# Rows by parity in a two-headed state-space kernel: 64x64 pieces for kv's first stage, half-width matmuls for A's last, loads in halves and a new order

## The chip, the core and the metric

The kernel runs on one core of a Trainium2 chip. The core has five engines with a queue each: TensorE (PE, with its weight loads shown apart as PEld), VectorE (DVE), ScalarE (ACT), GpSimd (POOL) and SyncE (SP). SP and POOL issue nearly all transfers here. The metric is the device time of one execution in microseconds.

## The reference

Two independent heads share the output's columns, the first 1024 from A and the last 1024 from B; each works on 2048 rows of 1024 columns in bf16.

```
k_shift = sum over t of k_pad[:, t:t+S, :] * shift_k[:, 3 - t]      # 4 taps along the rows
kv  = k_shift * v
y   = irfft(rfft(kv padded to 4096) * rfft(ssm_k padded to 4096))[:S]
A   = q * (y + kv * ssm_D)

Bu  = x @ B_bar^T                                                   # complex, 1024 states
h_t = Lam_bar * h_(t-1) + Bu_t                                      # 2048 steps
B   = 2 * Re(h @ C^T) + x * Dskip
```

## The kernel before

**Head B** goes through 16 chunks i of 128 rows. `x.i` loads a chunk transposed; `U.i.jp.jl` are PE's 16 matmuls of a quarter-pair of Bu into a PSUM bank, and `ue.i.jp` (L466, ACT) casts a bank to SBUF. VectorE then multiplies by a rotation table (`r1`, L479), adds (`r2`, L486), runs the recurrence as two scans (`sc`, L492), rotates back with `r3` (L479) and `r4` (L498). Between chunks `cy.i` (L488, ACT) copies the last column of chunk i-1, as r4 left it, into chunk i; the scans of chunk i wait for it. `y.i.dh.part` are PE's output matmuls, four of 512 columns (L508) and one of 128 with the diagonal Dd (L511) in each part, eight parts a chunk; `ye` (L517) casts them and `yst` or `ysp` stores them from POOL or SP. Before the first chunk, `bl`, `bT`, `bc` (L437) bring B transposed into BT, `cl`, `cT`, `cc` (L445) or `cx` bring C into CT, and `z1` (L362) and `z2` (L365 to L367) write the rotation tables Z1 and Z2 on ACT; only r3 reads Z2.

**Head A** is a convolution by a transform of 4096 points in three stages of small matmuls. For each of 16 row phases n2, `kvm`, `kva`, `kvb`, `kvc` (VectorE) make kv from k, the taps and v. k sits in a ring of eight row slots that `kp.r` fills, two rows a time; `vp.r` and `qp.r` load v and q likewise. `am.n2.dh` (L563) is kv's first stage, `ae` (L569) its cast, `ast.n2` (L572) its store to the scratch Ys_kv from POOL. The filter goes the same way through `hl`, `hT`, `hc`, `hm` (L609), `he`, `hst` into Ys_h. Stage two works on 32 frequency groups g in pairs i: `lh.i`, `lk.i` (L629) and `lw.i` load, `sh.g` and `sk.g` (L640) transform, `she` (L649) and `ske` (L656) cast, `sw` and `swp` (L660) swap partitions by DMA from POOL or SP, `pr.i` (L666, VectorE) multiplies, `sa.g` (L678) transforms back, `sae` casts, `vst` stores to Vs. A load lk or lh needs all first-stage stores of its scratch, since each reads rows of all of them. The last stage reads Vs with `vl.n2`, transforms with `a3.n2.dh` (L706), casts with `a3e` (ACT) or `a3ev` (VectorE, both L713), multiplies by q with `qm.r` (L715, VectorE) and stores with `ost` or `osp` (POOL or SP).

Row 16m + s of k, v, q and A's output lies on partition m in slot s. The first stage wants even and odd m apart (p = 0, 1); before the change this is done by constants whose other rows, or columns, are zero:

```
F1 = np.stack([tr * (m % 2 == p)[:, None] for p in range(2)], axis=1)
G = np.stack([tr.T * (m % 2 == p)[None, :] * 2 / NFFT for p in range(2)], axis=1)
```

`am` is then two full 128x128 matmuls of 512 columns, one for each p, and `a3` two of them that accumulate in one bank. The filter's `hm` runs already as four 64x64 matmuls (constant FQ), two row halves by two column halves.

All of this is issued in one order, written out as a string of words, each a step of the above with the arena slots (a), PSUM banks (p), scan slots (h) and weight slots (w) that it takes. Every engine and every DMA queue runs its own steps in the order of the words; semaphores do the rest. SBUF is one arena of 53 units, handed out by hand, and so are the eight banks.

```
cur.setdefault(code, []).append(int(n))
...
E[f](*map(int, args))
```

Of the kernel before, what the change touches and what calls it, by code (L numbers as in the profile page):

```python
# [32 lines left out]
def a_constants():  # L33
# [5 lines left out]
    F1 = np.stack([tr * (m % 2 == p)[:, None] for p in range(2)], axis=1)  # L39
    FQ = np.concatenate([tr[::2], tr[::2]], axis=0)  # L40
    G = np.stack([tr.T * (m % 2 == p)[None, :] * 2 / NFFT for p in range(2)], axis=1)
# [23 lines left out]
    return f(F1), f(FQ), f(G), f(W)  # L65

ORDER = """
bl.0.1:a46 ld_par ld_w:a0 wb.3:p0 wbe.3:a20 bl.6.0:a32 par_T:p2 p32 exp1 dd wb.6:p4 wbe.6 wb.2:p2 ld_F wbe.2 kp.0:a12
bl.7.1:a42 bl.6.1:a43 wb.1:p1 bl.0.0:a35 wb.7:p3 wbe.7 wbe.1 wb.0:p7 bT.6.0:p4 gz x.1:a48 kring bc.6.0 wbe.0
bl.7.0:a25 kp.1 wb.5:p1 wbe.5 wb.4:p5 bl.1.0:a9 bT.0.1:p4 dve2 dve3 tabA1:a4a40a6a10 wbe.4 exp2 kp.-1 bT.6.1:p1  # L70
bT.0.0:p2 x.0:a49 bc.0.1 bT.7.1:p3 bl.2.1:a42 sm_pre sin0 bT.7.0:p5 rt bc.6.1 bc.0.0 bl.3.1:a24 tabA2 bl.1.1:a33
kvm.3:a26 U.1.3.0:a34p6 bT.1.0:p4 par_rest kva.3 U.1.0.0:p2 bc.7.1 bc.7.0 U.1.3.1 U.0.3.0:a8p0 U.0.3.1 kvm.1:a44
bT.2.1:p5 sin2 bl.2.0:a43 bl.3.0:a50 sin1 bT.3.1:p7 eo bc.1.0 kvb.3:a39 bT.1.1:p3 U.0.0.0:p1 bc.2.1 bl.5.0:a30 kva.1
kvm.2:a0 stt bl.5.1:a31 kva.2 bT.2.0:p4 bl.4.1:a38 bc.1.1 bT.3.0:p5 bl.4.0:a52 ue.0.3 U.1.0.1 U.0.0.1 bc.2.0 bc.3.0
bT.4.1:p3 bT.5.0:p0 ue.1.0 bT.4.0:p5 kp.-2 U.1.1.0:p2 bc.3.1 kvm.0:a26 bT.5.1:p4 bc.5.0 bc.4.1 kvb.1:a38 kva.0 bc.4.0
cl.2.0:a32 bc.5.1 ue.0.0 U.1.1.1 U.0.1.0:p0 x.2:a51 cT.2.0:p7 kvb.2:a36 ue.1.3 U.0.1.1 U.0.2.0:p4 vp.0:a42 U.0.2.1
# [19 lines left out]
ye.2.0:a48 hst.0.6.0 he.0.7.0.0 vp.4:a10 sc.3.0 y.2.1.0:p6 y.2.1.1 am.3.1:p5p0 hst.0.4.1 ae.3.0.1 y.2.1.2 y.2.1.3
sc.3.1 hst.0.5.0 am.4.1:p2p4 x.5:a34 ae.4.1.1:a6 hst.0.7.0 ye.2.1 ae.3.1.1 U.4.0.0:a32p7 U.4.3.0:p5 am.5.1:p1p0
kvm.6:a0 U.4.3.1 ae.5.0.1:a28 vp.3:a40 U.4.0.1 kvc.8 ast.3 ue.4.3 am.4.0:p1p3 ue.4.0 ae.4.1.0 ae.5.1.1 r3.3:a44
U.4.2.0:p4 kva.6 am.5.0:p3p5 U.4.2.1 ae.5.0.0 ae.4.0.0 am.8.1:p7p6 ae.4.0.1 am.8.0:p0p3 ae.8.1.0:a4 U.4.1.0:p1 r4.3
kvb.6:a35 yst.2 hst.0.5.1 ue.4.2 kvc.6 U.4.1.1 ae.8.1.1 ae.8.0.1 U.5.1.0:a30p3 kvm.9:a46 U.5.1.1 ae.5.1.0 y.3.1.0:p2  # L100
y.3.0.0:p6 am.6.1:p4p5 ast.4 y.3.0.1 kvm.7:a24 ue.5.1 am.6.0:p7p3 ae.6.1.0:a6 ue.4.1 ae.8.0.0 ae.6.1.1 ae.6.0.1
y.3.0.2 kva.9 y.3.0.3 kva.7 y.3.1.1 hm.0.1.1:p3p1 he.0.1.1.1:a38 hm.0.1.0:p4p5 he.0.1.0.1 ye.3.0:a35 he.0.1.1.0
he.0.1.0.0 ae.6.0.0 y.3.1.2 kvb.9:a36 kvb.7:a51 kvc.9 hl.3.1:a42 y.3.1.3 hl.3.0 ye.3.1 hl.2.1:a0 hl.2.0 U.5.2.0:p1
am.9.1:p6p3 ae.9.0.1:a8 ae.9.1.1 U.5.2.1 ue.5.2 hT.1.3:p2 kvc.7 ast.5 hc.1.3:a50 kp.5 r1.4:a46 am.7.0:p6p5 hT.1.0:p7
hst.0.1.0 ae.7.0.0:a32 ae.7.1.0 ast.6 kvm.11:a24 ast.8 am.9.0:p0p4 ae.9.1.0 r2.4:h0 kva.11 hc.1.0:a28 hT.1.1:p1
hT.1.5:p6 am.7.1:p5p2 hc.1.1:a29 ae.7.1.1 cy.4 sc.4.0 kvb.11:a40 U.5.3.0:p3 ysp.3 hd.1 ae.7.0.1 U.5.0.0:p4 ae.9.0.0
ast.7 kvm.10:a24 hst.0.1.1 sc.4.1 U.5.0.1 U.5.3.1 hc.1.5:a41 hm.1.1.0:p5p2 kva.10 hm.1.1.1:p0p7 x.8:a11 ue.5.0 kp.6
x.9:a36 U.8.0.0:a6p1 he.1.1.1.0:a46 hT.1.4:p0 hT.1.7:p6 he.1.1.0.1 U.8.3.0:p4 ue.5.3 hc.1.4:a51 he.1.1.1.1 vp.5:a48
x.6:a10 he.1.1.0.0 U.8.3.1 kvc.11 hT.1.2:p0 hc.1.7:a29 hT.1.6:p3 hm.1.7.0:p7p5 kvb.10:a37 he.1.7.0.1:a32 he.1.7.0.0
hc.1.2:a3 U.8.1.0:p2 U.8.1.1 ue.8.3 r3.4:a42 U.8.0.1 am.11.0:p6p5 U.6.1.0:a38p7 ae.11.1.0:a4 U.6.1.1 hc.1.6:a35 ue.8.0  # L110
ae.11.0.0 am.11.1:p3p4 U.6.3.0:p0 ue.6.1 ast.9 hst.1.1.0 vp.6:a0 hst.1.1.1 ue.8.1 ae.11.1.1 U.6.3.1 ae.11.0.1 ast.11
kvm.12:a24 hm.1.0.0:p1p5 hm.1.2.0:p6p7 hm.1.7.1:p2p4 he.1.7.1.0 r4.4 U.6.0.0:p3 he.1.7.1.1 he.1.0.0.0:a46 kva.12
# [78 lines left out]
def full_kernel(ctx, tc, A_q, A_k, A_v, A_shift_k, A_ssm_k, A_ssm_D, B_x, B_Lre, B_Lim, B_Bre, B_Bim,  # L191
# [590 lines left out]
```

## Time and profile before

| | |
|---|---|
| three runs | 357.69, 358.66, 360.29 us (median 358.66) |
| profiled execution | 358.65 us, of which the span is 356.8 us |
| mean granted TensorE clock | 0.990 |
| PE / DVE / ACT / POOL busy | 333.2 / 330.3 / 271.5 / 68.9 us |
| moved by DMA | 100.91 MB, 283 GB/s over the span |

The span runs from the first to the last instruction; busy time is the union of an engine's instructions. In a row of the timeline the columns are start, length, engine, line, operation, output and inputs, count, and in brackets the idle time just before it with what ended it. Successive instructions of an engine overlap a little in the records, so a difference of starts tells better than a length what one more instruction costs. A row of the waits gives the waiting engine and line, what it waited for, and total, times and longest in us.

### The profile page before, as it was taken

How to read it: one execution, taken by the hardware profiler on the slowest of the kernel's cores; microseconds unless marked ns; L12 is line 12 of the kernel's file. 1: busy time of each engine (PE TensorE's matmuls, PEld its weight loads, DVE VectorE, ACT ScalarE, POOL GpSimd, SP SyncE). 2: the span in 40 equal slices, each digit the busy share in tenths (PEclk: the TensorE clock that was granted, in tenths of full speed). 3: DMA queues.
4: the chain of work that ended last, by engine and by line, in shares of the span. 5: the costliest groups of instructions: out<-in, count | busy, mean ns of one | idle time of the engine just before them, and what ended most of it. 6: DMA issues, size and time to landing. Idle time of an engine off the chain costs nothing.

```text
span 356.8 us, 9113 instructions
## 1 busy us (share of the span) xinstructions
PE 333.2 (93%) x3745; PEld 223.9 (63%) x3785; DVE 330.3 (93%) x277; ACT 271.5 (76%) x512; POOL 68.9 (19%) x108
## 2 busy tenths in 40 slices
PE   5869989899999979999999999999999999999993
PEld 1769989444775868658574574655474777844441
DVE  4999899799999999999969999999999999999980
ACT  5999799897558984889667688898898997226540
POOL 5000020231612210561200020022130412000021
PEclk9998999999999998999999999999999999999999
DMA  7999899671988994787979889999999899899694
GB/s 224 326 279 310 248 242 281 194 253 44 298 294 317 282 260 177 193 312 222 348 246 311 305 303 275 317 366 320 359 303 344 319 314 327 296 355 386 204 401 154
DMA packets 62565, 100.91 MB, mean 283 GB/s; under 512 B 29438, under 2 KB 31502, under 8 KB 62524
## 3 DMA queue, kind: packets, MB, share of 16 engines
q1 hardware_dynamic: 52684, 66.60, 62.0%
q0 software_dynamic: 9840, 33.74, 26.0%
q8 instruction: 29, 0.48, 0.6%
q14 instruction: 12, 0.10, 0.1%
HBM read 52.08 MB, written 33.55 MB: 240 GB/s over the span
## 4 chain that ended last, share of the span: by engine, by line
PE 70%; DMA 12%; ACT 7%; issue 5%; SPq 3%; POOL 1%; DVE 1%; POOLq 0%; DVEq 0%
PE bank L508 25%; PE bank L461 24%; PE bank L640 4%; PE bank L678 4%; DMA arena<-in_B_x_dram 3%; DMA wslot<-a_c_W 3%; PE bank L706 3%; PE bank L563 3%; SPq L443 3%; ACT BT L437 2%; PE bank L609 2%; PE bank L511 2%; DMA arena<-Vs 2%; DMA CT<-in_B_C_im_dram 2%; PE bank L421 1%
## 5 line engine op out<-in xcount | busy, mean ns | idle before, releaser
L461 PE MATMUL bank<-arena,BT 128*128 128x128 bf16 x2048 | 129.2, 222 | 5.1 <-DMA arena<-in_B_x_dram 3.5
L461 PEld LDWEIGHTS <-BT 128*128 128x128 bf16 x2048 | 120.1, 99 | 19.5 <-issue 7.7
L508 PE MATMUL bank<-CT,gslot 128*128 128x512 bf16 x483 | 120.5, 379 | 3.0 <-issue 1.0
L492 DVE TENSOR_TENSOR_SCAN gslot<-rtab,gslot 128x1040 bf16<-128x1040 f32 x32 | 73.0, 2312 | 6.3 <-ACT gslot L488 6.2
L508 PEld LDWEIGHTS <-gslot 128*128 128x128 bf16 x512 | 44.5, 98 | 53.0 <-issue 8.7
L466 ACT CAST arena<-bank 128x512 bf16<-128x512 f32 x64 | 38.7, 623 | 19.5 <-PE bank L461 17.5
L569 ACT CAST arena<-bank 128x512 bf16<-128x512 f32 x64 | 35.9, 620 | 8.9 <-PE bank L563 8.7
L617 ACT CAST arena<-bank 128x512 bf16<-128x512 f32 x64 | 34.3, 616 | 6.9 <-PE bank L609 5.9
L666 DVE TENSOR_TENSOR arena<-arena 128x4096 bf16<-128x4096 bf16 x16 | 36.6, 2287 | 2.1 <-DMA arena<-arena 1.0
L479 DVE TENSOR_TENSOR arena<-arena,Z 128x4096 bf16<-128x4096 bf16 x16 | 36.5, 2284 | 1.1 <-ACT arena L466 1.1
L479 DVE TENSOR_TENSOR arena<-gslot,Z 128x4096 bf16<-128x4096 bf16 x16 | 36.6, 2286 | 0.4
L686 ACT CAST arena<-bank 128x512 bf16<-128x512 f32 x60 | 33.4, 610 | 4.4 <-PE bank L678 4.3
L656 ACT CAST arena<-bank 128x512 bf16<-128x512 f32 x58 | 33.0, 614 | 2.6 <-PE bank L640 2.4
L649 ACT CAST arena<-bank 128x512 bf16<-128x512 f32 x57 | 31.5, 615 | 4.4 <-PE bank L640 4.4
L620 POOL DMA_DIRECT2D Ys_h<-arena x32 | 23.3, 730 | 45.8 <-ACT arena L617 45.8
L517 ACT CAST arena<-bank 128x512 bf16<-128x512 f32 x31 | 18.8, 606 | 15.6 <-PE bank L511 15.6
L543 DVE TENSOR_TENSOR arena<-arena 128x4096 bf16<-128x4096 bf16 (+3 forms) x16 | 30.1, 1884 | 0.4 <-ACT arena L466 0.3
L511 PE MATMUL bank<-Dd,arena 128*128 128x128 bf16 x128 | 28.0, 219 | 0.2
L572 POOL DMA_DIRECT2D Ys_kv<-arena x16 | 11.2, 719 | 84.2 <-ACT arena L569 82.2
L660 POOL DMA_DIRECT2D arena<-arena x16 | 8.8, 553 | 82.9 <-ACT arena L649 44.9
L713 ACT CAST arena<-bank 128x512 bf16<-128x512 f32 x24 | 12.8, 597 | 12.1 <-PE bank L706 10.9
L511 PEld LDWEIGHTS <-arena 128*128 128x128 bf16 x128 | 12.5, 98 | 15.1
(102 smaller groups left out, 383.3 us busy)
## 6 DMA issues: line engine op xcount, KB each, us to landing
Ys_kv<-arena POOLq DMA_DIRECT2D x16, 512.0 KB, 5.7
Ys_h<-arena POOLq DMA_DIRECT2D x32, 256.0 KB, 4.0
arena<-Ys_h SPq DMA_DIRECT2D x16, 512.0 KB, 5.7
arena<-Ys_kv SPq DMA_DIRECT2D x16, 512.0 KB, 6.1
Vs<-arena POOLq DMA_DIRECT2D x16, 512.0 KB, 5.5
arena<-Vs SPq DMA_DIRECT2D x16, 512.0 KB, 7.5
arena<-in_A_k_dram SPq DMA_DIRECT2D x8, 512.0 KB, 4.3
arena<-in_A_v_dram SPq DMA_DIRECT2D x8, 512.0 KB, 4.6
```

The costliest lines, as they stand in the source:

```text
L461: nc.tensor.matmul(pu[:, w, jl, :], BT[:, 2 * jp + jl, w, d, :], xT[:, d, :], start=(d == 0), stop=(d == ND - 1))
L466: either("ue", lambda cp, i, jp: cp(st["u", i][:, :, 2 * jp:2 * jp + 2, :], st.pop(("pu", i, jp))))
L479: nc.vector.tensor_mul(m, s_, win(Z))
L492: nc.vector.tensor_tensor_scan(gf, rtab[:].rearrange("p j t -> p (j t)"), gf, 0.0, ALU.mult, ALU.add)
L508: nc.tensor.matmul(py, h[:, w, j, 2:GW], CT[:, j, w, dh * 512:(dh + 1) * 512], start=(j == 0 and w == 0), stop=False)
L511: nc.tensor.matmul(py[:, part * P:(part + 1) * P], st["xT", i][:, d, :], Dd[:, d, :], start=False, stop=(part == 3))
L569: cp(st["ysb", n2][:, p, dh * 512:(dh + 1) * 512], st.pop(("pa", n2, p, dh)))
L617: cp(o, st.pop(("pb", hf, s, e, r)).rearrange("p (n c t) -> p n c t", n=2, c=2))
L649: cp(st["hab", i][:, 0, a, l, :], st.pop(("ps", "h", g, l)))
L656: cp(st["x16", i][:, a, l, :], st.pop(("ps", "k", g, l)))
L666: nc.vector.tensor_mul(hab, st.pop(("x16", i)).rearrange("p a l d -> p (a l d)").unsqueeze(1).to_broadcast([P, 2, 2 * D]), hab)
L686: cp(st["vsb", i][:, a, dh * 512:(dh + 1) * 512], st.pop(("pv", g, dh)))
```

## The change

k, v, q and A's output are addressed with the parity of m split off, so that partitions 0 to 63 hold the even and 64 to 127 the odd m:

```diff
-    kr, vr, qr, oar = (a.rearrange("(m s) d -> m s d", s=16) for a in (k, v, q, out_a))
+    kr, vr, qr, oar = (a.rearrange("(n p s) d -> n p s d", p=2, s=16) for a in (k, v, q, out_a))
-    G = np.stack([tr.T * (m % 2 == p)[None, :] * 2 / NFFT for p in range(2)], axis=1)
+    G = tr[::2].T * 2 / NFFT
+    def half(dma, t_, dr, r, p):
+        dma(t_[64 * p:64 * p + 64, :, :], dr[:, p, 2 * r:2 * r + 2, :])
...
+    for p_, e_ in enumerate("ab"):
+        for q_, dma_ in (("", spd), ("g", gpd)):
+            E["kp" + e_ + q_] = lambda r, p=p_, dma=dma_: kp(dma, r, p)
+            E["vp" + e_ + q_] = lambda r, p=p_, dma=dma_: row_pair("v", dma, vr, r, p)
+            E["qp" + e_ + q_] = lambda r, p=p_, dma=dma_: row_pair("qt", dma, qr, r, p)
...
+    def f1_quarters(outs, src):
+        for a in range(2):
+            for r in range(2):
+                rows, cols = slice(64 * r, 64 * r + 64), slice(64 * a, 64 * a + 64)
+                nc.tensor.matmul(outs[r][cols, :], FQt[rows, cols], src[rows], start=True, stop=True)
...
     def am(n2, dh):
+        outs = [bank(), bank()]
         for p in range(2):
-            st["pa", n2, p, dh] = bank()
-            nc.tensor.matmul(st["pa", n2, p, dh], F1t[:, p, :], st["kv", n2][:, dh * 512:(dh + 1) * 512], start=True, stop=True)
+            st["pa", n2, p, dh] = outs[p]
+        f1_quarters(outs, st["kv", n2][:, dh * 512:(dh + 1) * 512])
...
         for p in range(2):
-            nc.tensor.matmul(pt, Gt[:, p, :], st["vv", n2][:, p, dh * 512:(dh + 1) * 512], start=(p == 0), stop=(p == 1))
+            nc.tensor.matmul(pt[64 * p:64 * p + 64, :], Gt[:], st["vv", n2][:, p, dh * 512:(dh + 1) * 512], start=True, stop=True)
...
+    def ostore(dma, r):
+        for p in range(2):
+            dma(oar[:, p, 2 * r:2 * r + 2, :], st["ot", r][64 * p:64 * p + 64, :, :])
```

So am is four 64x64 matmuls as hm is, with the same constant; a3 is two matmuls of 128 rows and 64 columns, each into its half of a bank. Every load of k, v and q and every store of A's output is two DMAs of 64 partitions. A word now names the half and the queue: `kpa.2` is the even half of k's rows 4 and 5 from SP, `kpbg.2` the odd half from POOL. `kp.-2` loads one row in place of two. F1 and its load are gone (`ld_F` loads FQ, `ld_Q` is dropped). Of the 48 halves named in the words for r = 0 to 7, 24 go by POOL; y's stores go five times by SP and eleven by POOL (ten and six before). VectorE takes 5 of the a3 casts (8 before), 8 of sae (4), 4 of she (7), 4 of ske (6) and one of ue (none). There are also steps that bring x by other ways (`xs`, `xl`, `xn`, `xt`, `xc`); no word of the order uses them.

The order string is new from the first word to the last. Three places matter below.

ACT, from the last casts of B to the rotation tables, before (L466 is ue, L445 cc, L362 z1, L569 ae, L365 to L367 z2):

```order
L445 COPY CT_73<-bank7_100 128x8x128
L466 CAST arena_92<-bank0_93 128x2x256
L362 ACTIVATE Z1_74<-Z1_74 128x1024
L466 CAST arena_92<-bank4_97 128x2x256
L466 CAST arena_92<-bank1_94 128x2x256
L569 CAST arena_92<-bank5_98 128x512
L569 CAST arena_92<-bank6_99 128x512
L466 CAST arena_92<-bank3_96 128x2x256
L466 CAST arena_92<-bank2_95 128x2x256
L365 CAST Z2_75<-arena_92 128x1024
L366 CAST Z2_75<-arena_92 128x1024
L367 ACTIVATE Z2_75<-arena_92 128x1024
```

and with the change (L485 is ue, L435 bc, L361 z1, L364 to L366 z2, L607 ae):

```order
L435 ACTIVATE BT_72<-bank3_95 128x1024
L361 ACTIVATE Z1_74<-Z1_74 128x1024
L364 CAST Z2_75<-arena_91 128x1024
L365 CAST Z2_75<-arena_91 128x1024
L366 ACTIVATE Z2_75<-arena_91 128x1024
L485 CAST arena_91<-bank6_98 128x2x256
L485 CAST arena_91<-bank4_96 128x2x256
L485 CAST arena_91<-bank1_93 128x2x256
L485 CAST arena_91<-bank5_97 128x2x256
L485 CAST arena_91<-bank7_99 128x2x256
L607 CAST arena_91<-bank2_94 128x512
L485 CAST arena_91<-bank0_92 128x2x256
```

z2's three writes stood behind ue.0.2, the last cast that r1.0 needs (the row after z1); now they stand ahead of it, and five ue, chunk 0's four among them, follow them.

ACT around cy.7, the copy that the scans of chunk 7 wait for, before (L649 she, L466 ue, L488 cy, L656 ske):

```order
L649 CAST arena_92<-bank7_100 128x512
L649 CAST arena_92<-bank3_96 128x512
L649 CAST arena_92<-bank4_97 128x512
L466 CAST arena_92<-bank6_99 128x2x256
L649 CAST arena_92<-bank2_95 128x512
L488 COPY gslot0_86<-gslot2_88 128x16
L466 CAST arena_92<-bank1_94 128x2x256
L466 CAST arena_92<-bank5_98 128x2x256
L656 CAST arena_92<-bank6_99 128x512
```

and with the change (L536 ye, L691 ske, L684 she, L507 cy):

```order
L684 CAST arena_91<-bank7_99 128x512
L485 CAST arena_91<-bank0_92 128x2x256
L536 CAST arena_91<-bank2_94 128x512
L691 CAST arena_91<-bank0_92 128x512
L691 CAST arena_91<-bank7_99 128x512
L684 CAST arena_91<-bank3_95 128x512
L507 COPY gslot1_86<-gslot0_85 128x16
L684 CAST arena_91<-bank6_98 128x512
L684 CAST arena_91<-bank2_94 128x512
L536 CAST arena_91<-bank4_96 128x512
```

Right ahead of cy.7 stood four she and a ue of chunk 10; now ye.5.1, two casts ske of group 1 and a she do.

VectorE from r4.15 to its end, before (L498 r4, L715 qm, L713 a3ev, L517 ye):

```order
L498 TENSOR_TENSOR gslot1_87<-arena_92 128x16x128
L715 TENSOR_TENSOR arena_92<-arena_92 128x2048
L713 CAST arena_92<-bank7_100 128x512
L713 CAST arena_92<-bank6_99 128x512
L713 CAST arena_92<-bank0_93 128x512
L715 TENSOR_TENSOR arena_92<-arena_92 128x2048
L713 CAST arena_92<-bank5_98 128x512
L715 TENSOR_TENSOR arena_92<-arena_92 128x2048 x4
L713 CAST arena_92<-bank4_97 128x512
L715 TENSOR_TENSOR arena_92<-arena_92 128x2048
L517 CAST arena_92<-bank6_99 128x512
```

and with the change (L517 r4, L743 a3ev, L745 qm, L536 ye):

```order
L517 TENSOR_TENSOR gslot0_85<-arena_91 128x16x128
L743 CAST arena_91<-bank7_99 128x512
L743 CAST arena_91<-bank4_96 128x512
L743 CAST arena_91<-bank5_97 128x512
L745 TENSOR_TENSOR arena_91<-arena_91 128x2048 x3
L536 CAST arena_91<-bank1_93 128x512
```

Seven products qm followed the last rotation; three do now.

More of the change, by code (lines that the diff above doesn't have):

```diff
@@ L96 @@
[L96 to L110, printed above, removed]
```

300 lines of the change are left out of this document (163 added, 137 removed).

## The prediction

> **What bounds the kernel now.** The profiled execution took 358.65 us, of which 356.8 are the span and 1.85 lie around it; the median of the three runs shown is 358.66, so the sum below stands for both. I read the page's busy shares and slices first, then the busy time by stage.
>
> ```profile
> PE 333.2 (93%) x3745; PEld 223.9 (63%) x3785; DVE 330.3 (93%) x277; ACT 271.5 (76%) x512; POOL 68.9 (19%) x108
> ...
> PE   5869989899999979999999999999999999999993
> ...
> DVE  4999899799999999999969999999999999999980
> ...
> 260.00:300.00 40.00, 39.73 (x565) 27.65 (x568) 38.06 (x25) 36.77 (x75) 9.90 (x16) 1.00 0.93 320
> ...
> 340.00:350.00 10.00, 9.95 (x54) 4.80 (x53) 7.42 (x8) 3.43 (x7) 2.90 (x4) 1.00 1.01 392
> ```
>
> In the two stretches the columns are length, PE, PEld, DVE, ACT, POOL, clock, DMA share. TensorE and VectorE are both full from about 30 us until VectorE runs out near 347. Neither alone is the bound: a lighter PE pays only where VectorE was waiting for it, or where PE is alone, in the last 15 us. So the next view is what ended VectorE's idle time.
>
> ```profile
> DVE gslot L492 <- ACT gslot L488: 6.2, 6, 2.7
> ...
> DVE arena L666 <- DMA arena<-arena: 1.0, 2, 0.6
> ...
> DVE arena L666 <- ACT arena L656: 0.6, 1, 0.6
> ...
> DVE arena L543 <- ACT arena L466: 0.3, 1, 0.3
> DVE arena L556 <- PE bank L461: 0.3, 1, 0.3
> DVE arena L666 <- issue: 0.2, 1, 0.2
> DVE arena L649 <- ACT arena L686: 0.2, 1, 0.2
> ```
>
> These seven rows add up to 8.8 us, all of it between the first rotation r1.0 and the last one, r4.15 (total, times, longest). Most is the scan waiting for cy, a 0.3 us copy on ScalarE that itself stands behind casts waiting for PE.
>
> **The change, part by part. TensorE's pieces.** What four 64x64 pieces cost is in the trace already, since hm runs so before the change.
>
> ```profile
> 66.05 0.22 PE L511 MATMUL bank<-Dd,arena 128*128 128x128 bf16 x1
> 66.11 1.03 PE L508 MATMUL bank<-CT,gslot 128*128 128x512 bf16 x4
> 66.97 0.22 PE L511 MATMUL bank<-Dd,arena 128*128 128x128 bf16 x1
> 67.12 0.63 PE L609 MATMUL bank<-arena,FQt 64*64 64x512 bf16 x8
> 67.68 0.71 PE L587 MATMUL bank<-ident,arena 128*128 128x128 bf16 x8
> ...
> 71.48 0.59 PE L563 MATMUL bank<-arena,F1t 128*128 128x512 bf16 x2
> 71.91 1.03 PE L508 MATMUL bank<-CT,gslot 128*128 128x512 bf16 x4
> ...
> 73.85 0.84 PE L609 MATMUL bank<-arena,FQt 64*64 64x512 bf16 x12
> 74.62 0.61 PE L508 MATMUL bank<-CT,gslot 128*128 128x512 bf16 x2
> ```
>
> By starts: the old am (two full matmuls, L563) takes 71.91 - 71.48 = 0.43. Two hm take 67.68 - 67.12 = 0.56, three take 74.62 - 73.85 = 0.77, so one more costs 0.21 and a run of them 0.14 besides. Ahead of the run 67.12 - 66.97 = 0.15 pass where 66.11 - 66.05 = 0.06 do without a switch: 0.09 more. A run of tiled matmuls thus costs 0.23 beyond its pieces, and an am that stands alone costs 0.44 in place of 0.43: nothing is gained by quarters that don't stand beside others. Of the new half-width a3 (128 rows, 64 columns) no row exists. Its bounds are 0.43 (the two in turn, as now) and 0.21 (side by side); I take 0.21, because the nearest rows, the four pieces, already hold two streams on the same rows with different columns.
>
> Counted in the order, am and a3 are 32 each, and the tiled runs go from 49 to 81 (the new order puts am beside am, hm or sh, and a3 in runs of one to seven). So PE's work changes by 32 x (0.21 - 0.43) twice, -7.0 and -7.0, and by 32 x 0.23 = +7.4: together -6.7 us.
>
> The Trainium skill, "TensorEngine Tiling (Array Packing)", section Tiling Modes, says that changing the tiling mode drains TensorE. The trace agrees, at 0.23 us a run; leaving the drain out, PE would shed 14.1 us in place of 6.7. The same section lists 128x64 as two tiles that work independently, which no trace here shows; by it a3 costs the 0.21 taken, and without it PE's sum would be about zero.
>
> **The start.** VectorE's first rotation r1.0 waits for ScalarE's cast ue.0.2.
>
> ```profile
> 36.91 0.66 ACT L466 CAST arena<-bank 128x512 bf16<-128x512 f32 x1
> ...
> 37.60 2.29 DVE L479 TENSOR_TENSOR arena<-arena,Z 128x4096 bf16<-128x4096 bf16 x1 [1.11 <-ACT arena L466]
> ...
> 41.76 1.09 ACT L365 CAST Z<-arena 128x1024 bf16<-128x1024 f32 x1
> ...
> 44.62 1.04 ACT L445 COPY CT<-bank 128x1024 bf16<-128x1024 bf16 x1
> ```
>
> The new order has the three writes of Z2 ahead of that cast, 44.62 - 41.76 = 2.9 us, and one CT copy less, which by its row is as long as one of the three (1.04 to 1.09, overlapped): 0.9. Everything else ahead of it is the same in number. ScalarE is full there, so r1.0 comes 2.0 later: **+2.0**. It is more only if the x tiles, now seventeen and nineteen loads down SP's queue, come after about 25 us, since PE then has some 14 us of pieces to do ahead of ue.0.2.
>
> **VectorE from r1.0 to r4.15.** By the order four of the products qm that stood behind r4.15 now stand ahead of it, one cast fewer does, and one kvc has moved ahead of r1.0.
>
> ```profile
> 333.92 1.22 DVE L498 TENSOR_TENSOR gslot<-arena 128x2048 bf16<-128x2048 bf16 x1
> ...
> 336.19 1.28 DVE L713 CAST arena<-bank 128x512 bf16<-128x512 f32 x2
> ...
> 340.28 4.62 DVE L715 TENSOR_TENSOR arena<-arena 128x2048 bf16<-128x2048 bf16 x4
> ...
> 349.46 1.03 PE L508 MATMUL bank<-CT,gslot 128*128 128x512 bf16 x4
> ...
> 350.38 1.03 PE L508 MATMUL bank<-CT,gslot 128*128 128x512 bf16 x4
> ...
> 351.24 0.22 PE L511 MATMUL bank<-Dd,arena 128*128 128x128 bf16 x1
> ...
> 352.38 0.57 POOL L519 DMA_DIRECT2D out_dram<-arena  x1 [3.96 <-ACT arena L517]
> ```
>
> Four qm take 4.6, a cast 0.64, and kvc, of 1024 elements like the additions, about the same: 4.6 - 0.6 - 0.6 = **+3.4**.
>
> **VectorE's waits in between.** Add up the pieces in the order at the rates above, a y part at 0.92 and a U piece, sixteen matmuls, at 0.9.
>
> ```profile
> 156.68 0.89 PE bank L461 x16
> ```
>
> The PE work that must be done before each of the sixteen products pr (its sh and sk) now stands 3.4 us further ahead of VectorE's own work than before, on the mean. So waits behind PE shrink. I take off the longest wait for cy (2.7), since cy.7, before which it stood, no longer follows a cast of a U piece, and the two rows behind PE's U (0.3 and 0.3): **-3.3**. The bounds are 0, and -6.8 if only the rows of the swaps and of the cast L649 stay (1.0 + 0.6 + 0.2 + 0.2 = 2.0); the value lies nearer to the single waits that I can name.
>
> **The tail.** r4.15 ends at 335.14 and the span at 356.8: 21.7 us, in which VectorE still has seven qm, and PE y.14's second half besides all of y.15. In the new order three qm, three casts and ye follow, and on PE four a3 (0.8) and y.15's eight parts. A part takes 350.38 - 349.46 = 0.92, eight take 7.4; from the last Dd piece to the end it was 356.8 - 351.24 = 5.6. With 0.2 of signalling and 0.7 for an a3 that still waits for its load: 0.2 + 0.8 + 7.4 + 5.6 + 0.7 = 14.7, so **-7.0**. VectorE's own rest there (3 x 1.15 + 3 x 0.64 + 0.7 = 6.1) is hidden behind y.15.
>
> **What costs nothing.** k, v and q come as 256 KB halves, and half of them from POOL. POOL is busy 68.9 of 357; 29 half loads and, net of what goes, ten more stores, at 0.57 to 0.69 each (the rows of L519 above and L572 below), add some 25 us beside its waiting.
>
> ```profile
> arena<-in_A_k_dram SPq DMA_DIRECT2D x8, 512.0 KB, 4.3
> ...
> arena<-arena POOLq DMA_DIRECT2D x16, 256.0 KB, 3.7
> ```
>
> A half lands in 3.7 where the whole took 4.3, and the bytes stay. On POOL's queue a half now stands behind stores that wait for ScalarE (kpbg.2 behind ast.2, kpbg.4 behind ast.3), with kvm behind it; in the order these stand 4 to 7 us of VectorE's work ahead of their use. Uncovered, each costs its 3.7. Dropping ld_Q and the zero halves of F1 and G, and one row of kp.-2, changes nothing on the path.
>
> **The sum.** 358.65 + 2.0 + 3.4 - 3.3 - 7.0 = 353.75; I forecast **353.8 us**.
>
> **The rivals.** *None of the waits goes:* cy's wait may be a matter of its place on ScalarE's queue, not of PE. For it: the longest came that way, and cy.7 now has other casts ahead of it. Against it: the 3.4 us above. 353.8 + 3.3 = 357.1.
>
> *VectorE hardly waits:* only the 2.0 of the swaps and L649 stay. 353.8 - 3.5 = 350.3. Against it: cy.1, cy.2 and cy.3 still have less than 3 us of VectorE's work between r4 and the scan.
>
> *Slower: the turn to stage two.* The last store of kv's first stage, ast.13, must land before lk.0 can be read, lk.0 before sk.1 and its casts, and on ScalarE cy.7 now stands behind those casts; the scan sc.7 waits for cy.7.
>
> ```profile
> 185.97 4.54 DVE L492 TENSOR_TENSOR_SCAN gslot<-rtab,gslot 128x1040 bf16<-128x1040 f32 x2 [2.75 <-ACT gslot L488]
> ...
> L572 POOL DMA_DIRECT2D Ys_kv<-arena x5: 667/687/838, 162.2 to 173.5; - x5
> ...
> DMA to landing us min/median/max: 4.0/5.7/8.9
> ...
> L629 SPq DMA_DIRECT2D arena<-Ys_kv x16: 359/484/1382, 179.4 to 273.2; - x16
> ...
> DMA to landing us min/median/max: 4.8/6.1/8.9
> ```
>
> From ast.13's last cast to cy.7 this is 0.1 + 5.7 + 6.1, then 0.35 for sk.1, 1.65 for three casts and 0.3: 14.2. VectorE has from there r1.7, two scans, r2.7, r3.6, r4.6 and r1.8, 13.4 us of work, and starts it 0.6 later: at the medians it waits 0.2, at the longest landings 6.6. What speaks for those is that ast.12, ast.14, ast.10 and ast.13 are issued in a row with three loads lh among them, 3.7 MB in all, 11 us at the 320 GB/s of the row for 260 to 300 us; what speaks against it is that they are spread over 6 us of PE's work. With one landing 1.3 us beyond the longest, and the 0.6 behind PE not gained since PE stands at sk.1 too: 353.8 + 6.6 + 1.3 + 0.6 = 362.3. From a mean landing of 7 us on it costs its excess twice.
>
> *The half-width pairs don't pair:* a3 stays at 0.43, and in 320 to 350 us PE is 99% busy, so the 7.0 is lost there: 360.8.
>
> **How the numbers follow.** The forecast 0.40, with its own range of 350.5 to 357; no wait goes 0.21; hardly a wait 0.15; the turn 0.18; no pairing 0.06. What a measurement can tell from no change is about 1%, 3.6 us. Below 355.1 lie four fifths of the forecast's chance and the third case, 0.32 + 0.15 = 0.47; above 362.2 some two thirds of the turn, half of the last case and a little of the second, 0.12 + 0.03 + 0.01 = 0.16; between them 0.37. The range is 349 to 362.5: it leaves out the worse half of the turn, and some of the best of the third case.
>
> **What would show it.** Right: am beside hm at 0.21 more a piece, a3 likewise, PE busy about 326; r1.0 near 39.6; under 6 us of waits in VectorE's rows after it; r4.15 ending some 15 us before the span does. Wrong: r1.0 after 42, a wait of several us at sc.7 behind sk.1's casts, a3 at 0.43, or a last stretch in which PE waits for vl's loads.

## The result: slower by 1.4%, and the profile after

The changed kernel took 361.87 us (median of 20 runs, 357.12 to 364.87), the kernel before 357.8 (20 runs, 352.94 to 363.9). The ratio is 1.0139, with a 95% interval of 1.0107 to 1.0171: about 5 us slower, where 353.8 was forecast. Runs of one kernel scatter, and every ratio here is taken over those within 1.5% of that kernel's fastest alone, so it is not the ratio of the medians. The profiled execution took 361.94 us with a span of 360.2. The shares of the page, the transfer engines' slices and the two big queues:

```profile
PE 328.4 (91%) x3819; PEld 216.5 (60%) x3849; DVE 331.6 (92%) x274; ACT 271.7 (75%) x515; POOL 88.5 (25%) x145
...
DMA  6999999979998587997899899988999999899994
...
q1 hardware_dynamic: 50320, 58.35, 58.1%
q0 software_dynamic: 12384, 41.61, 35.2%
```

PE is lighter, as forecast (by how much these two pages can't tell, since both lack some of PE's records; more on this below). What stands out is the last two rows (packets, MB, share of 16 engines' span). Together the transfers fill 93.3% of 360.2 us, 336 us. Before the change the same two rows were these:

```profile
q1 hardware_dynamic: 52684, 66.60, 62.0%
q0 software_dynamic: 9840, 33.74, 26.0%
```

That is 88.0% of 356.8, 314 us, for the same 100 MB. The change made the transfers 22 us longer in engine time; the prediction counted their issues and their bytes, but not this.

Then VectorE's waits in the changed kernel:

```profile
DVE arena L701 <- DMA arena<-arena: 2.6, 5, 1.4
...
DVE arena L691 <- issue: 2.3, 1, 2.3
DVE arena L587 <- PE bank L595: 2.1, 1, 2.1
DVE arena L638 <- ACT arena L630: 1.9, 1, 1.9
...
DVE arena L743 <- PE bank L736: 1.0, 1, 1.0
DVE arena L587 <- PE bank L625: 0.9, 1, 0.9
...
DVE gslot L511 <- ACT gslot L507: 0.3, 1, 0.3
...
DVE arena L721 <- PE bank L713: 0.2, 1, 0.2
DVE arena L701 <- ACT arena L691: 0.2, 1, 0.2
```

The wait behind cy (L507), 6.2 us before, is 0.3: more of it went than the 2.7 that the forecast took off. New ones took its place, and these rows, all after r1.0, add up to 11.5 us where 5.5 were forecast. The timeline shows where they start and how the two ends went (POOL's store, ScalarE's cast and VectorE's rows):

```profile
39.91 2.29 DVE L498 TENSOR_TENSOR arena<-arena,Z 128x4096 bf16<-128x4096 bf16 x1 [1.16 <-ACT arena L485]
...
106.98 0.67 POOL L610 DMA_DIRECT2D Ys_kv<-arena  x1 [8.96 <-ACT arena L607]
...
115.20 2.05 ACT L607 CAST arena<-bank 128x512 bf16<-128x512 f32 x4 [3.40 <-DMA Ys_kv<-arena]
...
117.27 0.69 DVE L587 TENSOR_TENSOR arena<-arena 128x1024 bf16<-128x1024 bf16 x1 [2.12 <-PE bank L595]
...
127.29 0.59 DVE L638 TENSOR_TENSOR arena<-arena 1x256 bf16<-1x256 bf16 x2 [1.93 <-ACT arena L630]
...
343.26 1.22 DVE L517 TENSOR_TENSOR gslot<-arena 128x2048 bf16<-128x2048 bf16 x1
```

The store ast.4 is issued at 106.98. The cast ae.8.0.0 takes the arena slot 0 that this store reads, and starts when it has landed, 8.2 us later; PE's am.7 and VectorE's kvb.9 (L587) and hd.1 (L638) wait in turn. The second place is from 260 to 300 us:

```profile
100.00:140.00 40.00, 37.88 (x511) 29.63 (x511) 34.81 (x28) 32.19 (x58) 9.98 (x15) 0.96 0.86 265
260.00:300.00 40.00, 36.40 (x503) 24.10 (x499) 35.72 (x26) 33.52 (x69) 9.07 (x16) 1.00 1.00 305
```

VectorE (the fourth column) is busy 34.8 of 40 us in the first stretch and 35.7 in the second (38.06 before). In the second the transfer engines' share, the last number but one, is 1.00 at 305 GB/s; before it was 0.93 at 320. They were busier and moved less.

### The profile page after: what moved, and what is told of

It reads as the page before. It is cut to its first block, busy times and chain, and to the rows that moved or that the text cites. A ratio compares the mean times of both kernels' runs of the same rounds, so it can differ in the third digit from the quotient of the medians.

```text
span 360.2 us, 9335 instructions
## 1 busy us (share of the span) xinstructions
PE 328.4 (91%) x3819; PEld 216.5 (60%) x3849; DVE 331.6 (92%) x274; ACT 271.7 (75%) x515; POOL 88.5 (25%) x145
## 4 chain that ended last, share of the span: by engine, by line
PE 49%; DMA 20%; issue 17%; DVE 6%; SPq 3%; POOL 2%; ACT 1%; POOLq 0%; DVEq 0%; ACTq 0%
PE bank L527 19%; PE bank L479 16%; DMA arena<-in_B_B_im_dram 5%; DMA wslot<-a_c_W 4%; PE bank L675 4%; DMA Ys_kv<-arena 4%; DMA arena<-arena 3%; PE bank L713 3%; PE bank L595 2%; DMA arena<-Vs 2%; PE bank L736 2%; DVE gslot L511 2%; DMA Ys_h<-arena 2%; PE bank L625 1%; DVE arena L701 1%
## 5 line engine op out<-in xcount | busy, mean ns | idle before, releaser
L479 PE MATMUL bank<-arena,BT 128*128 128x128 bf16 x2048 | 125.8, 221 | 0.9 <-ACT BT L435 0.6
L479 PEld LDWEIGHTS <-BT 128*128 128x128 bf16 x2048 | 116.9, 98 | 13.9 <-issue 11.5
L527 PEld LDWEIGHTS <-gslot 128*128 128x128 bf16 x512 | 43.0, 98 | 55.2 <-issue 15.9
L485 ACT CAST arena<-bank 128x512 bf16<-128x512 f32 x63 | 37.7, 629 | 9.9 <-PE bank L479 9.7
L652 ACT CAST arena<-bank 128x512 bf16<-128x512 f32 x64 | 35.7, 640 | 10.2 <-PE bank L595 8.5
L607 ACT CAST arena<-bank 128x512 bf16<-128x512 f32 x64 | 34.9, 634 | 7.5 <-DMA Ys_kv<-arena 3.4
L684 ACT CAST arena<-bank 128x512 bf16<-128x512 f32 x60 | 33.6, 612 | 8.4 <-PE bank L675 8.4
L691 ACT CAST arena<-bank 128x512 bf16<-128x512 f32 x60 | 33.9, 618 | 6.0 <-PE bank L675 5.9
L498 DVE TENSOR_TENSOR arena<-arena,Z 128x4096 bf16<-128x4096 bf16 x16 | 36.5, 2283 | 1.3 <-ACT arena L485 1.2
L498 DVE TENSOR_TENSOR arena<-gslot,Z 128x4096 bf16<-128x4096 bf16 x16 | 36.6, 2288 | 0.3
L721 ACT CAST arena<-bank 128x512 bf16<-128x512 f32 x56 | 31.1, 623 | 3.7 <-PE bank L713 3.6
L536 ACT CAST arena<-bank 128x512 bf16<-128x512 f32 x31 | 19.0, 616 | 13.5 <-PE bank L530 10.5
L595 PE MATMUL bank<-arena,FQt 64*64 64x512 bf16 x256 | 21.2, 389 | 3.9 <-ACT arena L607 1.9
L419 PE MATMUL bank<-ident,arena 128*128 128x128 bf16 x192 | 16.6, 243 | 8.3 <-DMA arena<-in_B_B_im_dram 6.3
L675 PE MATMUL bank<-arena,wslot 64*64 64x512 bf16 x256 | 20.6, 387 | 2.9 <-DMA wslot<-a_c_W 2.9
```

The source lines that it names most:

```text
L479: nc.tensor.matmul(pu[:, w, jl, :], BT[:, 2 * jp + jl, w, d, :], xT[:, d, :], start=(d == 0), stop=(d == ND - 1))
L485: either("ue", lambda cp, i, jp: cp(st["u", i][:, :, 2 * jp:2 * jp + 2, :], st.pop(("pu", i, jp))))
L498: nc.vector.tensor_mul(m, s_, win(Z))
L527: nc.tensor.matmul(py, h[:, w, j, 2:GW], CT[:, j, w, dh * 512:(dh + 1) * 512], start=(j == 0 and w == 0), stop=False)
L607: cp(st["ysb", n2][:, p, dh * 512:(dh + 1) * 512], st.pop(("pa", n2, p, dh)))
L652: cp(o, st.pop(("pb", hf, s, e, r)).rearrange("p (n c t) -> p n c t", n=2, c=2))
```

## The experiments

Each is compared with the kernel before on the same chip, so ratios are what should be compared; 1% is about 3.6 us. I first held the new order's waits for the whole loss, with the steps (pieces, halves) harmless.

### The order or the steps: four combinations

*The new steps in the old order*:

```diff
 # the words of before, with these in place of kp.r, vp.r, qp.r (ld_Q dropped)
-kp.0:a12
+kpa.0:a12 kpb.0
```

> The changed kernel's steps (pieces, half-width a3, loads and stores in halves, all halves of k, v, q from SP) in the order of before. PE sheds 32 x 0.22 twice and gains 0.23 for each of 41 more tiled runs (90 for 49): 14.1 - 9.4 = 4.7 us less. Theory (the loss is the new order's waits at the arena's slots and behind the loads, the steps themselves cost nothing): the waits of VectorE stay as before, some 9 us, the tail loses up to 3 of its 21.7 us since a3 is half as long: 354 to 357.5, so not slower than before. Rival (the steps cost it: half transfers that land no sooner than whole ones, or the switches of mode): 360 to 362, as the changed kernel.

370.45 us, ratio 1.0399 (1.0313 to 1.0484), above the rival's range too. My theory fell at once: without the new order the steps cost 4%, some 14 us, not nothing.

*The old steps in the new order*:

```diff
 # the kernel before with the new words; a pair of halves is one whole load at the place of the first
-kpa.2 kpbg.2
+kp.2
```

> The steps of before (full am and a3, k, v and q each one whole load from SP at the place of the first half, whole stores) in the new order. PE has 32 x 0.22 twice more work than in the changed kernel and 20 tiled runs fewer (61 for 81): 14.1 - 4.6 = 9.5 more. Theory (the order costs it): at least the changed kernel's time, and more by a part of the 9.5: 362 to 368. Rival (the steps cost it, the order is as good as the old one): 356 to 359.

364.43 us, ratio 1.0255 (1.0179 to 1.0330). So each order suits its own steps: before 1, the new order alone 1.026, the new steps alone 1.040, both 1.014. The next two split the steps.

*The pieces undone*, in the new order with its halves:

```diff
-        f1_quarters(outs, st["kv", n2][:, dh * 512:(dh + 1) * 512])
+        for p in range(2):
+            nc.tensor.matmul(outs[p], F1t[:, p, :], st["kv", n2][:, dh * 512:(dh + 1) * 512], start=True, stop=True)
...
-            nc.tensor.matmul(pt[64 * p:64 * p + 64, :], Gt[:], st["vv", n2][:, p, dh * 512:(dh + 1) * 512], start=True, stop=True)
+            nc.tensor.matmul(pt, G2t[:, p, :], st["vv", n2][:, p, dh * 512:(dh + 1) * 512], start=(p == 0), stop=(p == 1))
```

> The changed kernel, order and halves included, with am as two full 128x128 matmuls (the constant's other rows zero) and a3 as two full ones that accumulate, as before the change: only the pieces are undone. PE has 9.5 us more (14.1 less 20 switches of 0.23). Theory (halves cost next to nothing in the new order, PE is the bound behind the slot waits): as the old steps in the new order, 363 to 366. Rival (halves cost some us there too): 367 to 371.

371.51 us, ratio 1.0412 (1.0361 to 1.0464): just above the rival's range. The pieces are worth 2.7%, nearly 10 us, in the changed kernel (1.0412 against 1.0139). And against the old steps in the new order (1.0255), where k, v, q move whole, the halves cost 1.5%.

*The halves alone*, in the old order with the old matmuls (the words of the first experiment, the matmuls of the last):

> The order and the matmuls of before, with k, v, q and A's output by parity and in halves, all halves of k, v and q from SP: only the halves are changed. The pieces in the old order took 370.5, with SP issuing two halves at 1.1 to 1.2 us where one load took 0.35, and the swaps from SP landing after 5.8 instead of 3.6. Theory (it is the halves that cost the old order): 366 to 371. Rival (it is the pieces and their switches of mode, 41 more in that order): 357 to 360.

369.04 us, ratio 1.0354 (1.0291 to 1.0417). The halves are nearly all of the 1.0399; the pieces add 0.4% there, which the intervals do not tell from nothing.

### What it is in a half

Two kernels that differ from the one before in the 24 loads of k, v and q alone, all from SP. *Two transfers of all partitions, one row each*:

```diff
-            spd(t_, kr[:, 2 * r:2 * r + 2, :])
+        for s_ in range(2):
+            spd(t_[:, s_:s_ + 1, :], dr[:, 2 * r + s_:2 * r + s_ + 1, :])
```

> The kernel before the change, with each of the 24 whole loads of k, v and q issued by SP as two transfers of 128 partitions and one row of 2 KB each: as many issues as the halves, but all partitions. Theory (it is the 64 partitions of a half that make it slow): within 3 us of the kernel before, 356 to 361, and the mean share of the transfer engines stays near 88%. Rival (it is the second issue on SP's queue, some 0.6 us each, which pushes the transposed loads of x and C back): 366 to 371, as with the halves (369.0).

*Two transfers of 64 partitions, both rows*:

```diff
-            spd(t_, kr[:, 2 * r:2 * r + 2, :])
+        for p in range(2):
+            spd(t_[64 * p:64 * p + 64, :, :], dr[64 * p:64 * p + 64, 2 * r:2 * r + 2, :])
```

> The kernel before the change, with each of the 24 whole loads of k, v and q issued by SP as two transfers of 64 partitions, rows in their old places (partitions 0 to 63 and 64 to 127, no parity), stores whole. Theory (64 partitions are slow, whatever rows they hold): 365 to 371. Rival 1 (parity matters, that is rows 64 KB apart in place of 32 KB): 356 to 361. Rival 2 (issues on SP): as the loads in two rows, whatever these take.

By rows 356.69 us, ratio 0.9984 (0.9932 to 1.0036); by partitions 366.27, ratio 1.0274 (1.0174 to 1.0375). As many issues of as many bytes cost nothing in one shape and 10 us in the other. It isn't SP's queue, and parity isn't needed for it. The queue's totals and a neighbour's landing, by rows:

```profile
q1 hardware_dynamic: 56140, 66.60, 62.7%
...
arena<-in_A_ssm_k_dram SPq DMA_DIRECT2D x8, 512.0 KB, 5.1
```

and by partitions:

```profile
q1 hardware_dynamic: 53068, 66.60, 65.7%
...
arena<-in_A_ssm_k_dram SPq DMA_DIRECT2D x8, 512.0 KB, 8.2
```

The same 66.60 MB take 62.7% of 354.7 us, 222 us, by rows, and 65.7% of 363.4 us, 239 us, by partitions. The loads of the filter, the same in both and issued beside them, land after 8.2 us in place of 5.1. The cost is hardly in the halves' own landing (k's after 5.0 us by rows and 5.4 by partitions) but in what else wants the transfer engines. VectorE's waits say the same; for k it waits 1.1 us in all by partitions. Its waits behind cy and for the swaps, by rows:

```profile
DVE gslot L492 <- ACT gslot L488: 6.2, 4, 4.7
...
DVE arena L670 <- DMA arena<-arena: 0.4, 1, 0.4
```

and by partitions:

```profile
DVE gslot L492 <- ACT gslot L488: 9.8, 5, 5.6
...
DVE arena L670 <- DMA arena<-arena: 3.6, 2, 3.2
```

The Trainium skill has the rule, in "SBUF — State Buffer", section Door 1: The DMA port swizzle: partitions 0 to 63 reach only half of the ports that a transfer of all 128 reaches, and two transfers to the two halves do not make up for it (section "Can I just issue two DMAs to hit both halves?"). The measurements agree: with 48 transfers in both kernels, those of 64 partitions take 16 us more engine time, 0.34 us for each half of 256 KB. The ports themselves no run here shows.

*Whole loads in the layout by parity*, in the changed kernel:

```diff
+    kw, vw, qw = (a.rearrange("(n p s) d -> p n s d", p=2, s=16) for a in (k, v, q))
+        spd(t_, dr[:, :, 2 * r:2 * r + 2, :])
```

> The changed kernel with k, v and q loaded as whole 512 KB transfers from SP, at the place of the half that SP issued (or of the first, where POOL issued both), in the same layout by parity; A's output still goes out in halves, all else as in the changed kernel. Theory (slots and places in the order): stays within 1.5 us of the changed kernel, 360.5 to 363. Rival (halves load the transfer engines: their share went from 88% to 93% of the span at equal bytes, the swaps from SP land after 5.2 instead of 3.6 and the stores of Ys_h after 5.5 instead of 4.0): the share falls back towards 88%, the swaps to about 4, and the time to 357.5 to 359.5.

553.55 us, ratio 1.5541 (1.5443 to 1.5639): both were wrong. These 24 transfers have an outermost dimension of 2 at their source. VectorE waited for k four times, 10 to 38.9 us each; from its waits:

```profile
DVE arena L574 <- DMA arena<-in_A_k_dram: 49.9, 3, 21.8
DVE arena L576 <- DMA arena<-in_A_k_dram: 38.9, 1, 38.9
```

By the Trainium skill, "DMA: Bandwidth & Descriptors", section Why a DMA increments its semaphore by 16 and not by 1, a transfer uses as many engines, at most 16, as divide the outermost dimensions on both sides; by that these would use 2. Waits of 10 to 39 us for loads of 512 KB fit that; how many engines ran was not seen. Written like this, the layout by parity cannot be loaded whole in one fast transfer.

### What the halves cost in the changed kernel

*The changed kernel with whole transfers in the old rows*. The pieces then take wrong rows for even and odd, so this prices the work only:

```diff
-    half(dma, st[nm, r], dr, r, p)
+    dma(st[nm, r], dr[:, 2 * r:2 * r + 2, :])          # dr = "(m s) d -> m s d"
```

> The changed kernel, its order, pieces and half-width a3, but k, v, q and A's output move whole, 128 partitions each, with the rows where the kernel before had them (so the rows that the pieces take for even and odd are not that: the output is not the reference's, the work is the same). A load is on SP's queue where SP issued one of its halves, else on POOL's. Theory (the transfers of 64 partitions are what the prediction missed): 352 to 356, near the 353.8 that it forecast, 0.985 to 0.995 of the kernel before. Rival (the loss is in the order alone, at the slots and the weights): 360 to 362, as the changed kernel.

354.73 us, ratio 0.9929 (0.9891 to 0.9967): the theory. The time is within 1 us of the 353.8 forecast, but as a ratio the gain is about half of the forecast's (the next section has this). From its page:

```profile
PE 330.5 (94%) x3849; PEld 217.5 (62%) x3849; DVE 330.5 (94%) x274; ACT 271.3 (77%) x515; POOL 75.0 (21%) x119
...
q1 hardware_dynamic: 51022, 61.88, 58.3%
q0 software_dynamic: 11152, 38.34, 30.3%
```

And from its timeline:

```profile
39.74 2.29 DVE L498 TENSOR_TENSOR arena<-arena,Z 128x4096 bf16<-128x4096 bf16 x1 [1.23 <-ACT arena L485]
...
112.42 2.05 ACT L607 CAST arena<-bank 128x512 bf16<-128x512 f32 x4 [2.94 <-DMA Ys_kv<-arena]
...
336.75 1.22 DVE L517 TENSOR_TENSOR gslot<-arena 128x2048 bf16<-128x2048 bf16 x1
```

The transfers take 88.6% of 352.4, 312 us; with halves it was 336, so 24 us for 64 halves (48 loads and 16 stores), 0.37 each. The halves cost the changed kernel 2.1% (1.0139 against 0.9929), 7.5 us. With them go half of their issues, a good part of them POOL's (busy 75.0 in place of 88.5), and some 3 MB move from POOL's queue to SP's. That issues alone cost nothing was shown on SP's queue, by rows; for POOL's no run tells the two apart.

*Two arena slots exchanged*, in the changed kernel with its halves:

```diff
-ae.8.0.0:a0   vpb.5:a48   U.8.3.0:a0p0    ae.10.0.0:a48
+ae.8.0.0:a48  vpb.5:a0    U.8.3.0:a48p0   ae.10.0.0:a0
```

> The changed kernel with the arena slots 0 and 48 exchanged for four tiles (ae.8's pair takes 48, vpb.5 takes 0, U.8 takes 48, ae.10 takes 0), no word moved. ae.8.0.0 then no longer waits for the landing of the store ast.4. Theory: ScalarE's 3.4 us there goes, and with it VectorE's waits at kvb.9 (2.1), hd.1 (1.9) and part of kvb.11's (0.9): 357.5 to 359.5, against 361.9. Rival (the waits come back behind the next cast or behind PE): 361 to 362.

356.75 us, ratio 1.0007 (0.9959 to 1.0054): 1.3% faster than the changed kernel, a little more than forecast. ScalarE goes through without a wait, and so does VectorE; the rows that were 115.20 and 117.27:

```profile
109.55 2.07 ACT L607 CAST arena<-bank 128x512 bf16<-128x512 f32 x4
...
114.59 0.68 DVE L587 TENSOR_TENSOR arena<-arena 128x1024 bf16<-128x1024 bf16 x1
```

*Both: whole transfers and the exchanged slots* (again not the reference's rows):

> The same with the exchanged slots. With the steps of before in the new order, whole loads, ScalarE still waited 1.8 us for the store ast.4 (3.4 with halves). Theory (the two causes overlap: the slot hurts because the store lands late): 0 to 3 us faster than without the exchange, less than the 5 us that it brought with halves. Rival (they are separate and add): 5 us faster, below 350.

353.05 us, ratio 0.9880 (0.9815 to 0.9945). With whole transfers the exchange brings 1.7 us, the theory, though the intervals do not tell it from nothing; with halves it brought 5. So the causes overlap. ScalarE's wait for the store is little shorter with whole transfers (2.94, in the rows above, for 3.40), but what VectorE loses behind it there is 0.5, at hd.1, in place of 4.0 (2.1 and 1.9); why it loses so much less was not settled.

### Repairs of the rest

All with the slots exchanged. *Eight half loads of q behind the last swap of pair 13*, since the weights lw.13 were issued among them:

```diff
-qpa.3:a14 sh.29 ... lw.13:w1 ... qpb.0 ... qpag.4 qpbg.6 qpbg.1 qpa.6 ... qpa.2 ... qpb.2 sw.13.0
+sh.29 ... lw.13:w1 ... sw.13.0 qpa.3:a14 qpb.0 qpag.4 qpbg.6 qpbg.1 qpa.6 qpa.2 qpb.2
```

> The kernel with the exchanged slots, and in its order eight half loads of q (qpa.3, qpb.0, qpag.4, qpbg.6, qpbg.1, qpa.6, qpa.2, qpb.2) moved behind sw.13.0, the last swap of group pair 13; nothing else moved. In the trace with the exchanged slots VectorE loses 5.8 of the 40 us from 260 to 300, 3.4 of them behind PE, which waits for the weights lw.13, issued among these loads. Theory (the loads of q hold up the weights and the swaps): lw.13 lands in 4 to 5 instead of some 7 us, 3 to 4.5 us of the waits go: 352 to 354. Rival (they only collide later, with the loads vl of the last stage, or lw.13 is bound by its slot): 356 to 358.

362.44 us, ratio 1.0163 (1.0117 to 1.0209): the rival, and worse than it. By stage, first with the slots exchanged alone:

```profile
260.00:300.00 40.00, 34.36 (x473) 22.37 (x476) 34.16 (x25) 31.34 (x64) 8.46 (x14) 1.00 1.00 298
300.00:340.00 40.00, 39.36 (x339) 21.92 (x336) 39.29 (x27) 19.54 (x40) 7.55 (x13) 1.00 0.98 331
```

and with the loads moved, with the row of PE that decides:

```profile
260.00:300.00 40.00, 37.39 (x511) 24.28 (x509) 36.84 (x27) 33.14 (x68) 9.38 (x16) 1.00 0.87 262
300.00:340.00 40.00, 32.94 (x267) 17.64 (x265) 30.18 (x20) 14.44 (x30) 2.08 (x4) 0.91 0.98 315
```

```profile
318.54 0.64 PE L736 MATMUL bank<-arena,Gt 128*64 128x512 bf16 x2 [6.93 <-DMA arena<-Vs]
```

From 260 to 300 VectorE gains 2.7 us (36.84 busy, 34.16 without the move), a little less than forecast, and from 300 to 340 it loses three times as much (30.18 for 39.29), behind the loads vl. The transfer engines have no room there (0.98): a load moved away from one waiter lands on the next.

*The same, and z2 back behind ue.0.2*:

> The kernel with the exchanged slots and the late loads of q, and z2 put back behind ue.0.2. Theory (the prediction's +2.0 at the start, found as 2.3): r1.0 starts 2 us earlier, near 37.8, and the end comes 2 us earlier than without this: 350 to 352. Rival (VectorE is then held up at r3.0, which reads Z2, or behind PE, and the gain at the start is given back): within 0.7 us of the kernel without it.

365.93 us, ratio 1.0251 (1.0203 to 1.0299), 0.9% slower than without it, which neither side had expected (the intervals just overlap). In its timeline r1.0 comes 1.3 us earlier than in the changed kernel, and the scans of chunk 1 wait 3.6 us:

```profile
38.65 2.28 DVE L498 TENSOR_TENSOR arena<-arena,Z 128x4096 bf16<-128x4096 bf16 x1
...
58.67 4.54 DVE L511 TENSOR_TENSOR_SCAN gslot<-rtab,gslot 128x1040 bf16<-128x1040 f32 x2 [3.56 <-ACT gslot L507]
```

Their cy.1 stands on ScalarE behind copies of CT, and PE's transposes for these waited 2.3 us for a load of C. Why that load came later here was not settled; the gain at the start, at least, could not be taken home this way.

*A fourth weight slot*, so that lw.13 need not wait for one:

```diff
-NWS = 3
+NWS = 4
-lw.14:w0 U.13.2.0 ... sa.31 lw.13:w1
+lw.14:w0 lw.13:w3 U.13.2.0 ... sa.31
```

> The kernel with the exchanged slots and a fourth weight slot (1280 B a partition), which lw.13 takes, issued right behind lw.14; no other word moved. In the trace with the exchanged slots PE waits 2.0 us for lw.13 and VectorE 3.4 us behind it. Theory (lw.13 is late because its slot frees late): VectorE's 3.4 go, no load of q is later than before: 353 to 355, or 0.989 to 0.995 of the kernel before. Rival (the transfer engines are full from 260 to 300 us, the wait moves to the swaps and the loads of the last stage): 356 to 358.

356.12 us, ratio 1.0032 (0.9986 to 1.0078): not told from the version without it (1.0007), or from before. VectorE's wait behind lw.13 went from 3.4 to 0.9. By stage:

```profile
260.00:300.00 40.00, 37.33 (x511) 24.37 (x509) 36.93 (x27) 33.37 (x68) 9.19 (x15) 1.00 1.02 310
300.00:340.00 40.00, 38.33 (x312) 20.48 (x310) 37.74 (x26) 18.48 (x38) 7.09 (x12) 1.00 0.96 324
```

2.8 us of VectorE's time come back in the first stretch, and 1.6 go in the second (39.29 without). A gain near 1 us is below what these runs resolve.

*k and v whole in their old rows, with full am* (F1 as before the change):

> The kernel with the exchanged slots, but k and v in their old layout and whole (from the queue of SP where SP issued one of the halves, else from POOL), and am as two full matmuls with the zeroed constant; q, A's output and a3 as in the change. PE has 4.5 us more (7.0 less 11 switches), the transfers lose 31 halves. Theory (halves of k and v cost about as much as am's pieces gain): 355 to 359, against 356.8 with both. Rival (these halves cost nothing, and the pieces' gain is lost): 360 to 363.

360.44 us, ratio 1.0106 (1.0024 to 1.0188): the rival. With the slots exchanged, am's pieces seem to be worth more than the halves of k and v cost.

*q and A's output whole in their old rows, with full a3*:

> The kernel with the exchanged slots, but q and A's output in their old layout and whole, and a3 as two full matmuls that accumulate; k, v and am as in the change. PE has 4.9 us more (7.0 less 9 switches), all of it in the last 50 us. In the trace with the exchanged slots VectorE lost 5.8 of the 40 us from 260 to 300 beside loads of q, with the transfer engines full. Theory (halves of q load the transfer engines there): the losses at 260 to 300 fall to 2 or 3 us and the last stage gets 4 to 5 longer: 356 to 360. Rival (whole loads collide just as much): 360 to 364.

358.46 us, ratio 1.0086 (1.0046 to 1.0126), as the theory had it; from 260 to 300 VectorE is busy 36.0 of 40 us, 34.2 with halves. For either pair, pieces with halves come out ahead of full matmuls with whole loads (1.0007 against 1.0106 and 1.0086, with intervals that just overlap), so no mixture gains. No version that computes the reference was faster than the kernel before.

## Why the prediction was wrong

**The step that failed** is "What costs nothing": that halves "cost nothing" because "a half lands in 3.7 where the whole took 4.3, and the bytes stay". The 3.7 is the row of the swaps, the wrong neighbour: they go from SBUF to SBUF, and their 64 partitions are every second one of all 128 (`q:P:2` in the code), where a half's are 64 side by side. Which of the two differences matters no run here shows. The halves of k landed later; from the changed kernel's transfers:

```profile
arena<-in_A_k_dram POOLq DMA_DIRECT2D x9, 256.0 KB, 5.9
...
arena<-in_A_k_dram SPq DMA_DIRECT2D x8, 256.0 KB, 5.8
```

But k's whole loads from SP, in the same order, landed after 6.0. A landing time is the wrong quantity where the engines are 88% busy: the cost fell on the other transfers, 22 to 24 us of engine time, 7.5 us of the end. The prediction named that price for a half left uncovered, 3.7 us, but made no rival of it, and the price of a half that is covered, by what it takes from the others, it did not ask for.

**The sum without that step**, from the kernel with whole transfers (r1.0 at 39.74, r4.15 from 336.75 to 337.97, a span of 352.4), comes out term by term against the one profiled run of before:

| term | forecast | whole transfers | changed kernel |
|---|---|---|---|
| r1.0 against 37.60 before | +2.0 | +2.1 | +2.3 |
| r1.0 to r4.15's end, 297.5 before | +0.1 | +0.7 (298.2) | +7.1 (304.6) |
| tail, 21.7 before | 14.7 | 14.4 | 15.7 |

That run, 358.65 us, was a long one for its kernel: the runs of before that the ratios use have a mean near 356. As a ratio the forecast is 353.8 to 358.65, 0.9865, which lies below the 0.9891 to 0.9967 of the whole transfers, so that the time fits better than the gain. With the slots exchanged besides, 0.9880 (0.9815 to 0.9945), the forecast's ratio lies within. The halves and the slot together account for the miss, as far as these intervals tell.

**VectorE's waits**: 5.5 were forecast, with whole transfers they are about 6 (2.1 for the swaps), with halves 11.5. That the sums agree is partly luck: the forecast left 3.5 of the 6.2 behind cy, where at most 0.3 remained, and other waits came. The waits for cy went, but not because TensorE is lighter. With the old full matmuls in the new order VectorE idles 0.3 us before all its scans (the last number):

```profile
L492 DVE TENSOR_TENSOR_SCAN gslot<-rtab,gslot 128x1040 bf16<-128x1040 f32 x32 | 73.2, 2312 | 0.3
```

and with the new steps in the old order it waits for cy even longer than before:

```profile
DVE gslot L511 <- ACT gslot L507: 12.0, 5, 6.2
```

So it is the order that did it. Whether because PE's work stands further ahead in it, as the prediction had it, or because cy stands behind other casts, was not told apart.

**TensorE** shed what was forecast. The pages of before and after do not show it, because records of matmuls are missing in both: x3745 beside 3785 weight loads, x3819 beside 3849. With whole transfers all 3849 are there, and so are all 3785 of the old matmuls in the kernel with loads by rows:

```profile
PE 337.0 (95%) x3785; PEld 224.1 (63%) x3785; DVE 329.5 (93%) x277; ACT 271.2 (76%) x512; POOL 68.9 (19%) x108
```

From 337.0 to 330.5 is 6.5 us, where 6.7 was forecast; the prediction's "about 326" started from the incomplete 333.2. That half-width pairs run side by side, which no row had shown, is now shown. From the changed kernel's timeline, five a3 and one, by starts:

```profile
332.67 1.27 PE L736 MATMUL bank<-arena,Gt 128*64 128x512 bf16 x10
333.87 1.04 PE L527 MATMUL bank<-CT,gslot 128*128 128x512 bf16 x4
...
339.84 0.41 PE L736 MATMUL bank<-arena,Gt 128*64 128x512 bf16 x2
340.18 1.03 PE L527 MATMUL bank<-CT,gslot 128*128 128x512 bf16 x4
```

Five take 1.20, one 0.34: one more costs 0.215, as taken (0.21), and a run 0.13 besides. The rival in which they don't pair is out.

**The turn to stage two**, the rival that I held for the slower end, did not come: no wait of VectorE's at sc.7. The slower result came from elsewhere, and its time, 362.3, fits by chance. (At its longest landings the wait adds up to 6.2 and not 6.6, which makes it 361.9.)

**What else the prediction left out**: it took its waits from the rows of before, and did not ask of the new order which arena slot is taken back while a store still reads it. That was 1.3% here, and the words alone show the place: ae.8.0.0 takes slot 0 thirty-one words behind ast.4.

## What to carry to other kernels

Splitting a transfer by partitions is not the same as splitting it by rows: where the transfer engines are nearly full, 64 partitions side by side cost some 0.35 us more of engine time for each 256 KB here, and the bill comes at other transfers' waiters. Price a change of transfers by the engines' time (share times span), not by its own landing. Before two busy times are compared, compare the counts of instructions behind them. When an order is new, list for each buffer that is reused what must still read it and how long that took to land; and expect a load that is moved out of a full stretch to land on the next waiter.

## What the runs showed of the hardware that I had not expected

- The same loads of k, v and q in 48 transfers: by rows (128 partitions, 2 KB each) 0.9984 of the time, by partitions (64, 4 KB each) 1.0274.
- A transfer whose source has an outermost dimension of 2 held VectorE up for 10 to 39 us at a time, and the kernel took 553.55 us in place of 361.87.
- Two 128x64 matmuls on the same rows and different columns run side by side: 0.215 us for a pair of 512 columns, where two full ones take 0.43.
